# Loading `w_down` with one row in fourteen dealt apart: 13 rows per partition over all DMA engines, half of the last rows over four engines

## The chip, the core and the metric

The kernel runs on one core of a Trainium2 chip. The core has a matrix engine (PE), a vector engine (DVE), a scalar engine (ACT), GpSimd (POOL) and SyncE (SP), which here issues nearly all transfers; 16 DMA engines move the data from HBM to the on-chip memory of 128 partitions. The metric is device time in microseconds: the median of several executions.

## The reference

One decoding step for two rows `x` of 512 values: a layer norm, then attention over the last 4096 keys of a cache with 32 heads on 8 key heads, beside a gated feed-forward layer of width 1792; both are added to `x`. All is float32.

```python
x = A_x
xn = _layernorm(x, axis=-1)
return x + _A_ref(xn, A_k_cache, A_v_cache, A_wq, A_wo) + _B_ref(xn, B_W_gate, B_W_up, B_W_down)
...
def _A_ref(x, k_cache, v_cache, wq, wo):
    W = min(4096, max(256, Sk // 4))
    q = (x @ wq) ...                                # 32 heads of 128
    k, v = the last W keys and values, each for 4 heads
    p = _softmax(q k^T * (Dh ** -0.5), axis=-1)
    return (p v) @ wo
def _B_ref(x, W_gate, W_up, W_down):
    gate = jnp.einsum("bsd,df->bsf", x, W_gate)
    up = jnp.einsum("bsd,df->bsf", x, W_up)
    gate = gate * (gate > 0)
    h = gate * up
    return jnp.einsum("bsf,fd->bsd", h, W_down)
```

`W_down` has 1792 rows of 512 values, that is 2 KB each and 3.5 MB in all.

## The kernel before

Every weight and every piece of the caches is read once, 95 MB in all. SP issues the loads in the order of use: `wq` in two transfers of 4 MB, `W_gate` (`wg`) and `W_up` (`wu`) of 3.5 MB, sixteen transfers of 4 MB for keys (`k`) and values (`v`), then `W_down` (`wd`), and `wo` in a transfer of 4 MB and pieces of 2 MB, 1 MB, 512 KB and twice 256 KB. They go into a ring of four buffers (`RING`), so a load is issued when the load four places earlier has been used. Each transfer has 128 partitions as its outermost size. All these loads stand in one queue (q1 in the profile), one behind the other on each DMA engine.

SP, like every engine, runs its instructions in order; the kernel places them by hand (`manual_schedule`), and waits are put in where a tile's or a semaphore's earlier use asks for them. Transfers take eight semaphores in turn (DMAHW0 to DMAHW7 in the listings below), so the ninth takes the first one's again, once that transfer is known to be complete.

Early on, PE projects `x` to the queries and to gate and up; DVE multiplies those to `hh`, with four blocks of 448 of the 1792 columns one below the other, each on 32 partitions, and transposes it in blocks of 32 × 32 into `hT`, which has partition, row within the partition, and batch row. PE then works through scores (L259), softmax and values (L324) for eight key and value pieces, while DVE transposes the keys (L252, `kT`). At the end, after the last values, 14 matmuls `yw_ps<-wd,hT` (L422) take one row per partition of `wd` each, against the column of `hT` with the same index; eight small matmuls and a copy by ACT make `oT` from the last heads, and the matmuls on `wo` follow, the last ones (L426) piece by piece as the `wo` pieces land. DVE copies the sum to `yo` (L453), and SP and ACT write one row of the output each (L456).

In `load_down`, partition p holds rows 14p to 14p+13 of `W_down`, 28 KB in one stretch. So the `hT` column of partition p and index k belongs to feed-forward column 14p+k.

Of the kernel before, what the change touches and what calls it, by code (L numbers as in the profile page):

```python
# [9 lines left out]
F32 = mybir.dt.float32  # L10
# [10 lines left out]
def kernel(  # L21
# [12 lines left out]
    nc = tc.nc  # L34
    P = 128
    B, _, D = x.shape
# [18 lines left out]
    FB = F // P  # L55
# [4 lines left out]
    ring = ctx.enter_context(tc.tile_pool(name="ring", bufs=RING))  # L60
# [8 lines left out]
    def load(name, src, shape):  # L69
        t = ring.tile(shape, F32, name=name, tag="ring")  # L70
        nc.sync.dma_start(t, src)
        return t
# [6 lines left out]
    def load_ff(w, name):  # L79
        return load(name, w.rearrange("(p k) f -> p k f", p=P), [P, KC, F])  # L80

    def load_down():
        return load("wd", w_down.rearrange("(p k) e -> p k e", p=P), [P, FB, D])

    def load_kv(cache, name, g, a):
        r, b = divmod(g, B)
# [35 lines left out]
    hT = const.tile([P, FB, 32], F32, name="hT")  # L122
# [54 lines left out]
    for kc in range(KC):  # L177
        m, k = divmod(kc, 2)
# [12 lines left out]
    for kc in range(KC):  # L191
        for r in range(R):
            for c in range(C):
                n = r * C + c
# [6 lines left out]
    for r in range(R):  # L201
# [7 lines left out]
        for m in range(NB):  # L209
            src = qt[32 * m:32 * m + 32, :, :, 0].rearrange("p i (t h) b -> p b t h i", h=2)  # L210
            for x in range(Q):
                d = qz[32 * x:32 * x + 32, r * B:r * B + B, m]
                dst = bass.AP(
                    tensor=d.tensor, offset=d.offset + x * TK,
                    ap=[d.ap[0], d.ap[1], [64 + REP, NP], [32, 2], [1, REP]],
# [16 lines left out]
    nc.vector.scalar_tensor_tensor(gr, gs, 0.0, gs, op0=ALU.is_gt, op1=ALU.mult)  # L232
    hh = work.tile([P, FQ], F32, name="hh", tag="qs")
    nc.vector.tensor_tensor(hh, gr, u_ps, op=ALU.mult)
    nc.vector.transpose(hT, hh.rearrange("p (w k) -> p k w", k=FB))

# [161 lines left out]
    g = NG - 1  # L400
    vin = [load_kv(v_cache, "v", g, a) for a in range(NP)]
    dw = load_down()


# [80 lines left out]
```

## Time and profile before

| what | value |
|---|---|
| median of 3 runs | 230.34 us (230.26 to 230.57) |
| profiled execution: time, span | 230.8 us, 228.4 us |
| loads in queue q1 | 3896 packets, 94.90 MB, 97.0% of 16 DMA engines' span |
| mean DMA rate | 416 GB/s |
| PE, DVE, ACT busy | 63%, 49%, 12% of the span |
| granted PE clock, mean | 0.821 |
| chain that ended last: DMA, DVE, PE | 60%, 21%, 13% of the span |

The profiled execution is one of its own, 0.46 us above the median; its span runs from the first to the last instruction. In the rows below times stand in us from the start of the span. A row of the chain gives start, duration and the engine or transfer; a row of the DMA queues gives packets, MB and the time of the packets as a share of 16 engines over the span or window; the count "under 512 B" in the row on packets is, for queue q1, that of the completion packets of 4 B with which each DMA engine ends its part of a transfer. q8 and q14 are instruction fetches, q10 the queue of the transfers that ACT issues.

### The profile page before, as it was taken

What the parts mean: (1) busy time and instruction counts of PE and PEld (TensorE: products, weight loads), DVE (VectorE), ACT (ScalarE), POOL (GpSimd) and SP (SyncE); (2) the same over time, 40 slices, a digit from 0 to 9 for tenths busy, and PEclk for the clock granted to TensorE, in tenths of its full rate; (3) what the DMA queues carried; (4) which work ended last, traced back from release to release, by engine and by line L of the source; (5) the groups of instructions that cost most, each with busy time, mean ns of one, the idle gap of its engine ahead of it and who ended that gap; (6) DMA issues with size and microseconds to landing.
All of it is one profiled execution on the core that took longest, in us unless ns stands there. A gap on an engine that the chain in (4) does not pass through costs nothing.

```text
span 228.4 us, 2114 instructions
## 1 busy us (share of the span) xinstructions
PE 143.5 (63%) x864; PEld 40.1 (18%) x864; DVE 112.4 (49%) x176; ACT 27.0 (12%) x72; POOL 3.7 (2%) x11
## 2 busy tenths in 40 slices
PE   0582927806674038957499196859928757868393
PEld 0530211201111001402013011101401201214011
DVE  2300043049894499865992594797069272120000
ACT  2000123000000720003500000700000160000001
POOL 6000000000000000000000000000000000000000
PEclk9999767795999557997759859767995995999589
DMA  7999999999999999999999999999999999999991
GB/s 276 459 413 412 472 402 422 448 453 419 413 455 442 396 448 445 407 430 453 425 410 453 436 407 442 429 430 425 448 430 419 439 430 418 440 419 448 399 387 44
DMA packets 3917, 95.04 MB, mean 416 GB/s; under 512 B 442, under 2 KB 450, under 8 KB 836
## 3 DMA queue, kind: packets, MB, share of 16 engines
q1 hardware_dynamic: 3896, 94.90, 97.0%
q8 instruction: 7, 0.11, 0.2%
q14 instruction: 2, 0.02, 0.0%
q10 hardware_dynamic: 12, 0.01, 0.0%
HBM read 94.90 MB, written 0.00 MB: 416 GB/s over the span
## 4 chain that ended last, share of the span: by engine, by line
DMA 60%; DVE 21%; PE 13%; ACT 2%; issue 1%; SPq 1%; DVEq 0%; ACTq 0%
DMA k<-in_A_k_cache_dram 39%; DVE kT L252 16%; DMA wo<-in_A_wo_dram 11%; DMA wq<-in_A_wq_dram 9%; PE s L259 5%; PE o L324 4%; PE q_ps L195 2%; DVE pt L304 2%; ACT pz L291 1%; DVE pT L297 1%; DVE on L333 1%; PE oa L344 1%; SPq L441 1%; DVE m L271 1%; ACT L291 1%
## 5 line engine op out<-in xcount | busy, mean ns | idle before, releaser
L259 PE MATMUL s<-kT,qz 128*32 128x512 f32 x256 | 61.5, 780 | 43.7 <-DVE kT L252 43.7
L252 DVE STREAM_TRANSPOSE kT<-k 128x1024 f32<-128x1024 f32 x64 | 73.5, 1210 | 19.9 <-DMA k<-in_A_k_cache_dram 19.8
L324 PE MATMUL o<-v,pt 128*32 128x512 f32 x256 | 36.6, 677 | 0.0
L259 PEld LDWEIGHTS s<-kT,qz 128*32 128x32 f32 x256 | 10.7, 127 | 88.3 <-DVE kT L252 47.5
L344 PE MATMUL oa<-on,pick 128*16 128x512 f32 x16 | 12.5, 876 | 4.5 <-DVE on L333 4.5
L291 ACT ACTIVATE pz<-s,nm 64x512 f32<-64x512 f32 x8 | 5.8, 726 | 74.6 <-DVE nm L285 74.5
L195 PE MATMUL q_ps<-wq,xnT 128*32 128x512 f32 x64 | 10.9, 846 | 4.9 <-DMA wq<-in_A_wq_dram 4.9
L324 PEld LDWEIGHTS o<-v,pt 128*32 128x32 f32 x256 | 10.5, 122 | 19.9 <-issue 19.7
L304 ACT COPY pt<-pT 32x256 f32<-32x256 f32 x32 | 12.8, 401 | 5.6 <-DVE pT L297 5.2
L217 DVE COPY qz<-qt 32x32 f32<-32x32 f32 x16 | 3.0, 188 | 21.1 <-ACT qz L217 21.1
L422 PE MATMUL yw_ps<-wo,oT 128*2 128x512 f32 x56 | 8.1, 730 | 4.4 <-DMA wo<-in_A_wo_dram 4.4
L333 DVE TENSOR_TENSOR on<-o,own_u 128x512 f32<-128x512 f32 x8 | 5.4, 673 | 10.8 <-PE o L324 10.8
L453 DVE COPY yo<-y_ps 128x128 f32<-128x128 f32 x1 | 0.3, 292 | 20.2 <-PE y_ps L426 20.2
L304 DVE COPY pt<-pT 32x256 f32<-32x256 f32 x32 | 9.1, 285 | 0.5
L297 DVE STREAM_TRANSPOSE pT<-pz 128x1024 f32<-128x1024 f32 x4 | 5.0, 1246 | 8.3 <-ACT pz L291 8.3
L183 PE MATMUL xt_ps<-rep,xc 2*128 2x32 f32 x16 | 3.7, 402 | 8.4 <-DVE rep L176 8.4
L271 DVE TENSOR_REDUCE m<-s 128x1 f32<-128x512 f32 x4 | 2.8, 692 | 8.5 <-PE s L259 8.5
L225 PE MATMUL u_ps<-wu,xnT 128*32 128x448 f32 x32 | 4.8, 764 | 2.2 <-DMA wu<-in_B_W_up_dram 2.2
L291 ACT ACT_TABLE_LOAD x1 | 1.3, 1283 | 34.6 <-DVE nm L285 34.6
L183 PEld LDWEIGHTS xt_ps<-rep,xc 2*128 2x128 f32 x16 | 3.6, 319 | 8.4 <-DVE rep L176 8.4
L225 PE MATMUL g_ps<-wg,xnT 128*32 128x448 f32 x32 | 5.0, 783 | 0.0
L195 PEld LDWEIGHTS q_ps<-wq,xnT 128*32 128x32 f32 x64 | 2.7, 147 | 12.1 <-issue 6.2
(69 smaller groups left out, 56.5 us busy)
## 6 DMA issues: line engine op xcount, KB each, us to landing
k<-in_A_k_cache_dram SPq DMA_DIRECT2D x8, 4096.0 KB, 29.5
v<-in_A_v_cache_dram SPq DMA_DIRECT2D x8, 4096.0 KB, 29.2
wq<-in_A_wq_dram SPq DMA_DIRECT2D x2, 4096.0 KB, 16.7
wo<-in_A_wo_dram SPq DMA_DIRECT2D x1, 4096.0 KB, 29.7
wg<-in_B_W_gate_dram SPq DMA_DIRECT2D x1, 3584.0 KB, 29.4
wu<-in_B_W_up_dram SPq DMA_DIRECT2D x1, 3584.0 KB
wd<-in_B_W_down_dram SPq DMA_DIRECT2D x1, 3584.0 KB
wo<-in_A_wo_dram SPq DMA_DIRECT2D x1, 2048.0 KB, 22.9
```

Source lines behind the costliest of these rows:

```text
L183: nc.tensor.matmul(xt_ps[:, v, kc, :], lhsT, rep16.rearrange("r s b -> r (s b)"), start=True, stop=True)
L195: nc.tensor.matmul(q_ps[r][32 * c:32 * c + 32, :], xnT[:, 0, kc, :], wqt[kc // 2][:, kc % 2, n * 512:(n + 1) * 512], start=(kc == 0), stop ...
L225: nc.tensor.matmul(dst[32 * c:32 * c + 32, :], xnT[:, 1, kc, :], wt[:, kc, c * FQ:(c + 1) * FQ], start=(kc == 0), stop=(kc == KC - 1),)
L252: nc.vector.transpose(kt[:, c * n:(c + 1) * n].rearrange("p j m i -> p j (m i)"), src[:, c * n:(c + 1) * n])
L259: nc.tensor.matmul(ss[g][32 * q:32 * q + 32, :], qz[:, g, 2 * mh + m, a, h], kt[:, JS * s1:JS * s1 + JS, m, h::2], start=(a == 0 and mh == ...
L291: nc.scalar.activation(pv[o, :, :, h], ss[g][o].rearrange("p (j i) -> p j i", j=JS), AF.Exp, bias=nm[o], scale=SCALE, accum_out=l[o],)
L297: nc.vector.transpose(pT.rearrange("p j x t k -> p (j x t k)"), pz.rearrange("p j s -> p (j s)"))
L304: (nc.vector.tensor_copy if n % 2 else nc.scalar.copy)(pts[g][32 * x:32 * x + 32, :, s1, :, h], pT[q:q + 32, :, x].rearrange("p j t k -> p ...
L324: nc.tensor.matmul(o[32 * q:32 * q + 32, :], pts[g][:, a, s1, j:j + 4].rearrange("p u h k -> p (u h k)"), v[:, lo:lo + 512], start=(s1 == ...
L333: nc.vector.tensor_tensor(ons[a], o.rearrange("p (u d) -> p u d", u=4), own_u[:, :, None].to_broadcast([P, 4, P]), op=ALU.mult)
L344: nc.tensor.matmul(oa[g].rearrange("h u d -> h (u d)"), pick[:, 8 - 8 * a:24 - 8 * a], ons[a].rearrange("p u d -> p (u d)"), start=(a == 0 ...
L422: nc.tensor.matmul(yw_ps[32 * c:32 * c + B, :], lhsT, w, start=(n < Q), stop=(n >= wide - Q))
```

## The change

`W_down` is seen as 32 runs of 56 rows; four partitions share one run. Each partition gets 13 rows in one stretch (26 KB) from the first 52 rows of its run, by a transfer over 128 partitions. The last four rows of a run go to its four partitions, one each. These last rows come by five more transfers: four of 4 runs (16 rows, 32 KB in all, each with outermost size 4), and one of 16 runs (64 rows, 128 KB, outermost size 16). The bytes stay the same. The transpose of `hh` becomes two, one for the 13 rows and one for the last, to match.

```diff
+    FM = FB - 1
+    PR = 4
+    RUN = PR * FB
+
     def load_down():
-        return load("wd", w_down.rearrange("(p k) e -> p k e", p=P), [P, FB, D])
+        t = ring.tile([P, FB, D], F32, name="wd", tag="ring")
+        nc.sync.dma_start(
+            t[:, 0:FM], bass.AP(tensor=w_down.tensor, offset=w_down.offset, ap=[[RUN * D, P // PR], [FM * D, PR], [1, FM * D]])
+        )
+        n = 0
+        for m in [4] * 4 + [16]:
+            src = bass.AP(
+                tensor=w_down.tensor, offset=w_down.offset + (n * RUN + PR * FM) * D, ap=[[RUN * D, m], [D, PR], [1, D]]
+            )
+            nc.sync.dma_start(t[n * PR:(n + m) * PR, FM], src)
+            n += m
+        return t
...
-    nc.vector.transpose(hT, hh.rearrange("p (w k) -> p k w", k=FB))
+    hr = hh.rearrange("p (i n) -> p i n", n=RUN)
+    nc.vector.transpose(
+        hT[:, 0:FM].rearrange("p k (i j) -> p k i j", j=PR), hr[:, :, 0:PR * FM].rearrange("p i (j k) -> p k i j", k=FM)
+    )
+    nc.vector.transpose(hT[:, FM].rearrange("p (i j) -> p i j", j=PR), hr[:, :, PR * FM:RUN])
```

On SP, from the last two `v` loads to the output's write, this stood before (line, operation, tile and source, shape, and in brackets the semaphores waited for: DMAHW0 to DMAHW7 of earlier transfers, PE and DVE of those engines' work):

```order
L71 DMA v_0_798<-in_A_v_cache_dram 128x1x8192 [waits DMAHW7_49,DVE_49]
L71 DMA v_1_800<-in_A_v_cache_dram 128x1x8192 [waits DMAHW0_49,PE_49]
L71 DMA wd<-in_B_W_down_dram 128x7168 [waits DMAHW1_49,DVE_49]
L441 DMA wo_884<-in_A_wo_dram 128x8192 [waits DMAHW2_49,PE_49]
L441 DMA wo_886<-in_A_wo_dram 128x4096 [waits DMAHW3_49,PE_49]
L441 DMA wo_886<-in_A_wo_dram 128x2048
L441 DMA wo_886<-in_A_wo_dram 128x1024
L441 DMA wo_886<-in_A_wo_dram 128x512 x2
L456 DMA out_dram<-yo 4x128 [waits DMAHW5_49,DVE_49]
```

On SP in the same place, after the change:

```order
L71 DMA v_0_799<-in_A_v_cache_dram 128x1x8192 [waits DMAHW7_49,DVE_49]
L71 DMA v_1_801<-in_A_v_cache_dram 128x1x8192 [waits DMAHW0_49,PE_49]
L88 DMA wd<-in_B_W_down_dram 128x1x6656 [waits DMAHW1_49,DVE_49]
L96 DMA wd<-in_B_W_down_dram 16x1x512 x4
L96 DMA wd<-in_B_W_down_dram 64x1x512 [waits DMAHW2_49]
L460 DMA wo_890<-in_A_wo_dram 128x8192 [waits DMAHW3_49,PE_49]
L460 DMA wo_892<-in_A_wo_dram 128x4096 [waits DMAHW4_49,PE_49]
L460 DMA wo_892<-in_A_wo_dram 128x2048 [waits DMAHW5_49]
L460 DMA wo_892<-in_A_wo_dram 128x1024 [waits DMAHW6_49]
L460 DMA wo_892<-in_A_wo_dram 128x512 [waits DMAHW7_49]
L460 DMA wo_892<-in_A_wo_dram 128x512 [waits DMAHW0_49]
```

Five transfers have come in behind the first one of `wd`, and with five more semaphores taken the `wo` transfers now wait for the completion of the last two `v` loads (DMAHW3, DMAHW4), and the last four pieces for that of the large `wd` transfer (DMAHW5) and of its first three small ones (DMAHW6, DMAHW7, DMAHW0).

On PE, at the end, from the last softmax sum to the first matmuls on `wo`, after the change:

```order
L332 MATMUL lp_859<-l_749,by_h 16x1
L441 MATMUL yw_ps<-wd,hT 2x512 [waits DMAHW5_49]
L441 MATMUL yw_ps<-wd,hT 2x512 x12
L441 MATMUL yw_ps<-wd,hT 2x512 [waits DMAHW6_49,DMAHW2_49,DMAHW7_49,DMAHW1_49,DMAHW0_49]
L381 MATMUL op_880<-osb_793,spread 128x32 [waits DVE_49]
L381 MATMUL op_880<-osb_793,spread 128x32 x7
L441 MATMUL yw_ps<-wo_890,oT 2x512 [waits DMAHW3_49]
```

Before, the first of the 14 matmuls on `wd` waited for the one transfer and the other 13 for none; now the last of them waits for the five small transfers. On DVE the one transpose into `hT` is two, in the same place.

## The prediction

> **What bounds the kernel now.** I read the page's queues and chain first, then the chain in order of time at its end, then the DMA share in narrow windows.
>
> ```profile
> q1 hardware_dynamic: 3896, 94.90, 97.0%
> DMA 60%; DVE 21%; PE 13%; ACT 2%; issue 1%; SPq 1%; DVEq 0%; ACTq 0%
> 198.46 26.13 DMA wo<-in_A_wo_dram
> 224.59 0.04 issue
> 224.64 0.45 PE y_ps L426 x8
> 225.11 0.29 DVE yo L453
> ```
>
> Queue q1 (all loads) keeps the 16 DMA engines busy for 97.0% of the span, and the chain ends in the landing of the last piece of `wo`, with only 0.45 us of PE and 0.29 us of DVE before the output's write. So the end is set by the DMA engine that finishes its share last. The chain's DVE and PE shares lie earlier, where queued loads keep the engines fed. The windows at the end say how uneven the engines are (columns: window, its length, busy us of PE, PEld, DVE, ACT, POOL, clock, DMA share, GB/s).
>
> ```profile
> 222.10:222.60 0.50, 0.50 (x8) 0.11 (x8) 0.00 (x0) 0.00 (x0) 0.00 (x0) 1.00 0.78 303
> 222.60:223.10 0.50, 0.50 (x8) 0.00 (x0) 0.00 (x0) 0.00 (x0) 0.00 (x0) 1.00 0.48 184
> 223.50:224.00 0.50, 0.50 (x24) 0.29 (x16) 0.00 (x0) 0.30 (x1) 0.00 (x0) 1.00 0.38 147
> 224.20:224.70 0.50, 0.33 (x16) 0.06 (x8) 0.00 (x0) 0.00 (x0) 0.00 (x0) 1.00 0.00 0
> ```
>
> Share times 16 is engines at work: 0.48 is eight, 0.38 is six, and after 224.2 none. Six engines finish some 1.8 us after the first eight. Every load through q1 is cut evenly over 16 engines, so something else made six late. Next, the DMA view in narrow windows: each engine ends its part of a transfer with one tiny completion packet (the column "under 512 B"), so counting these tells when engines finish. Windows 36.8 to 37.9, 38.5 to 39.2 and 40.3 to 40.6 (the end of `wu`), then 202.3 to 203, 203.3 to 203.8 and 203.8 to 204.7 (the end of `wd`), then the page's rows of other queues:
>
> ```profile
> q8 instruction: 1, 0.02, 5.9%
> DMA packets 30, 0.49 MB, mean 702 GB/s; under 512 B 15, under 2 KB 15, under 8 KB 15
> DMA packets 3, 0.07 MB, mean 218 GB/s; under 512 B 1, under 2 KB 1, under 8 KB 1
> ...
> DMA packets 22, 0.42 MB, mean 603 GB/s; under 512 B 8, under 2 KB 8, under 8 KB 8
> DMA packets 11, 0.27 MB, mean 549 GB/s; under 512 B 2, under 2 KB 2, under 8 KB 2
> DMA packets 18, 0.39 MB, mean 437 GB/s; under 512 B 6, under 2 KB 6, under 8 KB 6
> ...
> q8 instruction: 7, 0.11, 0.2%
> q14 instruction: 2, 0.02, 0.0%
> ```
>
> The instruction fetch takes 5.9% of 16 engines for 1.1 us, that is 1.04 us of one engine, and behind it fifteen engines end `wu` in time and one over a microsecond late. A late engine never catches up, since all carry equal bytes. By the end of `wd`: eight in time, two from 203.3 on, six from 203.8 on. Of the seven q8 fetches one comes after 224.2 (window 224.2 to 226.6, row below); six before it and six late engines, two q14 fetches and two middling ones: every fetch met another engine.
>
> ```profile
> q8 instruction: 1, 0.02, 2.6%
> ```
>
> [...]
>
> **The change, part by part.** The price of bytes comes from the steady stretch 27.9 to 60.4, that of a 2 KB packet from 223.5 to 224.0, whether a small transfer uses few engines from the page's q10.
>
> ```profile
> q1 hardware_dynamic: 511, 13.99, 100.0%
> DMA packets 38, 0.07 MB, mean 147 GB/s; under 512 B 2, under 2 KB 2, under 8 KB 38
> q1 hardware_dynamic: 38, 0.07, 38.0%
> q10 hardware_dynamic: 12, 0.01, 0.0%
> ```
>
> *Removed on every engine.* The large transfer carries 13 rows per partition instead of 14: 2 KB less on each of the eight partitions of an engine, 16,384 B. 13.99 MB in 32.5 us over 16 engines is 26.9 GB/s each, so 0.61 us less.
>
> *Added on every engine.* The transfer of 16 runs brings 64 rows, four per engine. 38.0% of 16 engines for 0.5 us is 3.04 us, for 36 data packets and two completions: at most 84 ns per 2 KB. Four: 0.34 us. Net 0.27 us less on twelve engines.
>
> *Added on four engines.* Four transfers of 16 rows, if each runs on four engines, bring 16 rows to each: 16 × 84 ns = 1.34 us. Net of the first two terms, 1.1 us more. No row shows a load of outer size 4, but q10 comes near: its 12 packets are ACT's load of `x` (2 rows) and its store of 4 rows, each row with one completion, so outer size 2 used two engines and 4 used four. The bounds of a row are 76 ns (2,048 B at 26.9 GB/s) and 84 ns; I take 84, of the same size. If an engine stopped between pieces, it would be dearer (third rival).
>
> *Which four.* No view numbers the engines. I take it that a transfer starts them in the order of their numbers, so the lowest are those that start and finish first. In windows 11.97 to 12.19 (end of the first load), 202.43 to 202.67 (end of `wd`) and 222.12 to 222.34 (last piece) the first four completions stand:
>
> ```profile
> DMA packets 8, 0.13 MB, mean 596 GB/s; under 512 B 4, under 2 KB 4, under 8 KB 4
> DMA packets 10, 0.19 MB, mean 785 GB/s; under 512 B 4, under 2 KB 4, under 8 KB 4
> DMA packets 32, 0.07 MB, mean 326 GB/s; under 512 B 4, under 2 KB 4, under 8 KB 32
> ```
>
> Four in the first 0.22 us at the start, four in the first 0.24 us after all fetches: the leaders kept their lead, so none of the four first starters was met. [...]
>
> *Sum.* Twelve engines: 224.2 − 0.27 = 223.93 for the six late ones. The four: the latest of them completes before 222.34, plus 1.1 = 223.45. The late ones still end last, 0.48 us behind the four, and the chain behind the landing is unchanged: the profiled 230.8 (span 228.4 and 2.4 around it) becomes 230.53. It lies 0.46 above the median, so the median 230.34 becomes 230.07; I say 230.1. Even with ideal balance only 0.27 us can come, since the late engines lose no more.
>
> *SP's queue.* Five more issues, and waits for older transfers whose semaphores are taken again.
>
> ```profile
> 177.09 0.34 SPq L71 DMA_DIRECT2D wd<-in_B_W_down_dram  x1
> 185.00 0.33 SPq L441 DMA_DIRECT2D wo<-in_A_wo_dram  x1
> 196.67 2.23 SPq L441 DMA_DIRECT2D wo<-in_A_wo_dram  x5
> SPq L441 <- PE o L324: 17.4, 2, 9.9
> DVE kT L252 <- DMA k<-in_A_k_cache_dram: 19.8, 4, 8.7
> ```
>
> Five issues of 0.43 us (2.23 / 5 is 0.45 with gaps) are 2.2 us, inside the 7.6 us in which SP waits before 185.0. Then the first `wo` transfer waits for the second-last load of `v` as well, whose stragglers complete by about 186.4 (their `wd` end, 204.7 at most, less one 4 MB load of 9.75 us and one `wd` of 8.53 us, both from bytes at 26.9 GB/s): 1.4 us later, with `v` and `wd` still queued, so free. The four last `wo` pieces are now held until the parts of `wd` landed, about 204.6 instead of 197 to 199. At that moment each engine holds most of the 32 KB packets of the first `wo` transfer (9.7 us) and the 2 MB piece (4.9 us), issued before: the next piece is needed after 217. Cover about 12 us; without it every microsecond of wait would be one of idle engines.
>
> *PE and DVE.* The last matmul on `wd` waits for five transfers more. Queued behind it are the eight `op` matmuls and ACT's copy, which have room before the `wo` wait, and the transpose to `hT` becomes two in front of the first `kT`:
>
> ```profile
> PE yw_ps L422 <- DMA wo<-in_A_wo_dram: 4.4, 2, 4.1
> 46.51 0.94 DVE L235 STREAM_TRANSPOSE hT<-hh 128x448 f32<-128x448 f32 x1
> 50.66 1.25 DVE L252 STREAM_TRANSPOSE kT<-k 128x1024 f32<-128x1024 f32 x1 [3.21 <-DMA k<-in_A_k_cache_dram]
> ```
>
> The four engines end `wd` at 202.67 + 1.1 = 203.8, ahead of the late ones, so PE starts no later; and 4.1 us lie free before `wo`. The transposes may take from 0.9 to four times as long before the 3.21 us of idle DVE is used up. Both cost nothing.
>
> **Rivals.** *First, one of the four lowest engines is a late one* (engines start in another order, or the fetches meet other engines in each execution). Then 224.2 + 1.1 = 225.3 sets the end, 1.1 us later: 231.4. An early engine may end as late as 223.1 now before 1.1 us more costs time; past that it decides. Against it: the leaders' windows; for it, that start order is all I have for numbers, and one execution. With a middling engine, which ends by 223.5, 224.6 at most: 230.4 to 230.7.
>
> [...]
>
> *Third, small pieces do not stream.* If the four engines stop after each for as long as from the last packet to PE's release (224.2 to 224.6, 0.4 us), five stops add 2.0 to 223.45: 225.45, hence 231.6. Against it stands window 221.4 to 222.2, in which 2 KB pieces and 17 completions passed and the engines stayed full:
>
> ```profile
> q1 hardware_dynamic: 134, 0.31, 100.6%
> ```
>
> [...]
>
> *Fourth, the four-run transfers go over all engines*, one row each: −0.61 + 8 × 0.084 = 0.06 more everywhere, with completions 0.1: 230.4. Against it: q10.
>
> **How the numbers follow.** Forecast 0.64, own range 229.8 to 230.5 (the 0.27 and the ±0.2 of the shown runs). Late engine among the four, or level engines, 0.23; a middling one 0.05; pieces that stop 0.02; all engines 0.03; something else that is faster 0.03. A measurement here tells 0.2%, 0.46 us, from no change, and the forecast's 0.27 is less. Faster: 0.03 and the forecast's edge 0.06. Slower: 0.25. The rest is same. Leaving out the first rival would leave out more than 2 in 10, so the range reaches to 231.5.
>
> **What would show it.** In the trace after: the last engines done at 223.9 instead of 224.2; about twelve of 16 at work from 222.6 to 223.1 (eight before); the last completions of `wd`'s small pieces near 203.8; SP's last four `wo` issues after 204, with a DMA share of 1.0 up to 222. Wrong would be: a last landing near 225.3 with four engines or fewer at work ahead of it, a dip in the share near 217, or a seventh instruction fetch that moves before 223.5 and meets an engine still loading.

## The result, and the profile after

The changed kernel takes 232.05 us (median of 6, 231.88 to 232.58) against 230.44 us (median of 6) before: a ratio of 1.0072, interval 1.0059 to 1.0085, that is 1.6 us slower. The prediction had 230.1 and a range up to 231.5. The profiled execution took 232.21 us, with a span of 230.1.

The chain in order of time still ends in the landing of the last `wo` piece, now at 226.25 instead of 224.59; what follows it is as long as before:

```profile
206.82 19.43 DMA wo<-in_A_wo_dram
226.29 0.45 PE y_ps L445 x8
226.76 0.29 DVE yo L472
```

The windows of the end (DMA share in the column before the last):

```profile
222.60:223.10 0.50, 0.50 (x12) 0.10 (x4) 0.00 (x0) 0.00 (x0) 0.00 (x0) 1.00 1.01 397
223.50:224.00 0.50, 0.50 (x8) 0.11 (x8) 0.00 (x0) 0.00 (x0) 0.00 (x0) 1.00 0.63 246
225.00:225.50 0.50, 0.48 (x16) 0.32 (x16) 0.00 (x0) 0.49 (x1) 0.00 (x0) 1.00 0.20 78
225.50:226.00 0.50, 0.50 (x24) 0.31 (x16) 0.00 (x0) 0.00 (x0) 0.00 (x0) 1.00 0.04 16
```

Before, eight engines were at work from 222.6 to 223.1 (share 0.48); now all sixteen are (1.01). Everything is late, the early engines too. Where that happened is seen in one window, 202.5 to 206.0, in which the end of `wd` passes. First before, then after:

```profile
202.50:206.00 3.50, 1.95 (x16) 0.55 (x20) 1.18 (x4) 0.00 (x0) 0.00 (x0) 1.00 1.01 428
...
202.50:206.00 3.50, 1.00 (x12) 0.25 (x13) 1.02 (x3) 0.00 (x0) 0.00 (x0) 1.00 1.02 310
```

The DMA share is full in both (1.01 and 1.02), and the rate has fallen from 428 to 310 GB/s. The engines are as busy as ever, and each byte takes longer. (428 − 310) GB/s × 3.5 us is 0.41 MB not moved, or 0.96 us of the whole stream in this window alone. From 207 on the rate is normal again (418 GB/s in 207 to 222, 410 before in 207 to 221).

Durations of single packets, read from the trace's records (all pieces of 2 KB between 200 and 210; packets of 32 KB that started between 203 and 205):

```
kernel                                     2 KB: count, mean, longest ns    32 KB: count, mean, longest ns
before                                       -                              19, 1239, 1687 (one beside a fetch)
after                                      128, 114, 169                    12, 1773, 1844
one transfer of 128 partitions             128,  84,  95                    20, 1226, 1247
two transfers of 64 partitions             128, 110, 232                    16, 1506, 1742
four pieces to partitions 0-15, 32-47       64,  85,  93                    22, 1219, 1246
two pieces to partitions 0-31, 32-63        64,  84,  86                    23, 1223, 1241
four pieces to partitions 64-79, 96-111     64, 148, 194                    12, 2178, 2339
four pieces to partitions 16-31, 48-63      64, 148, 187                    12, 2003, 2216
```

The pieces cost 114 ns on average after the change, not 84, and the 32 KB packets of the first `wo` transfer, which the change does not touch, took 1.77 us on average while the pieces passed; before, those that started in the same two microseconds took 1.24 (1.21 without the one beside a fetch).

### The profile page after: what moved, and what is told of

It is laid out like the page before. It is cut to its first block, busy times and chain, and to the rows that moved or that the text cites. A ratio compares the mean times of both kernels' runs of the same rounds, so it can differ in the third digit from the quotient of the medians.

```text
span 230.1 us, 2122 instructions
## 1 busy us (share of the span) xinstructions
PE 136.0 (59%) x864; PEld 39.2 (17%) x864; DVE 112.3 (49%) x177; ACT 27.1 (12%) x72; POOL 3.7 (2%) x11
## 4 chain that ended last, share of the span: by engine, by line
DMA 69%; DVE 21%; PE 6%; ACT 1%; issue 1%; SPq 1%; DVEq 0%; ACTq 0%
DMA k<-in_A_k_cache_dram 39%; DVE kT L271 17%; DMA wd<-in_B_W_down_dram 12%; DMA wq<-in_A_wq_dram 9%; DMA wo<-in_A_wo_dram 8%; PE q_ps L210 2%; PE s L278 2%; PE o L343 2%; DVE pt L323 1%; DVE on L352 1%; ACT pz L310 1%; ACT L310 1%; DVE pT L316 1%; SPq L460 1%; DVE m L290 0%
## 5 line engine op out<-in xcount | busy, mean ns | idle before, releaser
L278 PE MATMUL s<-kT,qz 128*32 128x512 f32 x256 | 60.8, 765 | 49.2 <-DVE kT L271 49.2
L343 PE MATMUL o<-v,pt 128*32 128x512 f32 x256 | 33.0, 616 | 0.0
L210 PE MATMUL q_ps<-wq,xnT 128*32 128x512 f32 x64 | 10.4, 808 | 5.7 <-DMA wq<-in_A_wq_dram 5.7
L363 PE MATMUL oa<-on,pick 128*16 128x512 f32 x16 | 10.6, 750 | 4.5 <-DVE on L352 4.5
L441 PE MATMUL yw_ps<-wd,hT 128*2 128x512 f32 x28 | 3.6, 592 | 2.5 <-DMA wd<-in_B_W_down_dram 2.5
L240 PE MATMUL u_ps<-wu,xnT 128*32 128x448 f32 x32 | 3.2, 542 | 2.9 <-DMA wu<-in_B_W_up_dram 2.9
```

What stands on the lines that cost most here:

```text
L210: nc.tensor.matmul(q_ps[r][32 * c:32 * c + 32, :], xnT[:, 0, kc, :], wqt[kc // 2][:, kc % 2, n * 512:(n + 1) * 512], start=(kc == 0), stop ...
L240: nc.tensor.matmul(dst[32 * c:32 * c + 32, :], xnT[:, 1, kc, :], wt[:, kc, c * FQ:(c + 1) * FQ], start=(kc == 0), stop=(kc == KC - 1),)
L278: nc.tensor.matmul(ss[g][32 * q:32 * q + 32, :], qz[:, g, 2 * mh + m, a, h], kt[:, JS * s1:JS * s1 + JS, m, h::2], start=(a == 0 and mh == ...
L343: nc.tensor.matmul(o[32 * q:32 * q + 32, :], pts[g][:, a, s1, j:j + 4].rearrange("p u h k -> p (u h k)"), v[:, lo:lo + 512], start=(s1 == ...
L363: nc.tensor.matmul(oa[g].rearrange("h u d -> h (u d)"), pick[:, 8 - 8 * a:24 - 8 * a], ons[a].rearrange("p u d -> p (u d)"), start=(a == 0 ...
L441: nc.tensor.matmul(yw_ps[32 * c:32 * c + B, :], lhsT, w, start=(n < Q), stop=(n >= wide - Q))
```

## Experiments

Two theories stood after this. *Crossing*: a transfer over 128 partitions would give each DMA engine certain partitions, a smaller transfer would give an engine other ones, and two engines would write the same part of the on-chip memory at once. *Rows*: 2 KB rows at a distance of 114,688 B, or the 26 KB stretches, are slow to read. A third, *four*: nothing but four engines with more to carry. Six kernels with times tell them apart; four runs of three more kernels, with marks, tell which engines are early. No run shows which engine writes which partition, nor an engine's number: which partitions belong to which engine, and what crosses, is the theory's, in the expectations as below, and the "lowest" engines are those that a small transfer uses. The four kernels with two or four pieces compute other sums over `wd`, as their expectations say; the loads are what counts.

**One transfer of 128 partitions for the last rows**

```diff
-        for m in [4] * 4 + [16]:
+        for m in [32]:
```

> The last rows come by one transfer over all 128 partitions instead of five small ones; everything else as after the change. Theory 'crossing' (the small transfers write partitions that in a 128-partition load belong to another DMA engine, and two engines on one place slow each other and their neighbours): nothing crosses here, so before's time plus about 0.1 us, 230.5, and no dip of the rate near 203 to 206. Theory 'rows' (2 KB rows out of a stretch of 114,688 B, or the 26 KB stretches, read slowly wherever they go): the dip stays, 231.5 to 232. Theory 'four' (the four engines are simply late, nothing else): 230.5.

230.45 us against 230.37, ratio 1.000 (0.9991 to 1.001). The 128 rows are the same 2 KB rows from the same places, the 13-row stretches and the two transposes too, and nothing is lost. In the window 202.5 to 206.0:

```profile
202.50:206.00 3.50, 1.48 (x16) 0.42 (x20) 0.66 (x2) 0.00 (x0) 0.00 (x0) 1.00 1.10 463
```

*Rows* falls.

**Two transfers of 64 partitions, each over all engines**

```diff
-        for m in [4] * 4 + [16]:
+        for m in [16, 16]:
```

> The last rows come by two transfers of 64 partitions, each over all 16 engines, four rows per engine each; no transfer over four engines. [...] 'Rows': 231.5 to 232. 'Four': no engine has more than another, 230.5.

231.28 us against 230.37, ratio 1.0033 (1.002 to 1.0047). No engine carries more than another: in the changed kernel the packets under 512 B are 32 more than before, 474 against 442, as four completions for each transfer of 16 rows and 16 for the one of 64 make it. Still it is slower, with a dip:

```profile
202.50:206.00 3.50, 1.96 (x16) 0.55 (x20) 1.63 (x4) 0.00 (x0) 0.00 (x0) 1.00 1.07 355
```

*Four* alone cannot explain this.

**Four pieces over four engines, written to partitions 0 to 15 and 32 to 47**

```diff
+    PIECES = ((0, 14), (32, 14), (0, 15), (32, 15))     # first partition, column of the tile
+    MAIN = FB * D - D // 2                              # 13.5 rows
...
+        for n, (p0, col) in enumerate(PIECES):
+            src = bass.AP(
+                tensor=w_down.tensor, offset=w_down.offset + (n * 4 * 56 + 52) * D, ap=[[56 * D, 4], [D, 4], [1, D]]
+            )
+            nc.sync.dma_start(t[p0:p0 + 16, col], src)
```

> The kernel before with its w_down transfer cut to 13.5 rows per partition, and four pieces of 16 rows over the four lowest engines behind it, written to partitions 0 to 15 and 32 to 47 (its sums over w_down are not the reference's; the bytes and the order of the loads are those of the changed kernel). 'Crossing': these partitions are the four engines' own, no dip; twelve engines carry 0.30 us less and four 1.04 us more: 230.1 if the four are early ones, 231.4 if one of them had an instruction fetch. 'Rows': a dip as after the change, over 231.5. 'Four': 231.4 to 232.

230.53 us against 230.37, ratio 1.0006 (0.9997 to 1.0015): between the two values that were expected, and the packets keep their durations, 85 ns and 1.22 us. The rate in the window is 400 GB/s, at a share of 0.94. Followed record by record (each packet starts on its engine 4 to some 15 ns before the recorded end of the one ahead of it), five of the six late engines end at 223.62 to 223.99, earlier than the 224.04 to 224.18 of before, but the sixth at 224.20 and the last engine with pieces at 224.42.

**The same, written to partitions 64 to 79 and 96 to 111**

```diff
-    PIECES = ((0, 14), (32, 14), (0, 15), (32, 15))
+    PIECES = ((64, 14), (96, 14), (64, 15), (96, 15))
```

> As the run with partitions 0 to 15 and 32 to 47, with the four pieces written to partitions 64 to 79 and 96 to 111 (sums over w_down not the reference's). 'Crossing': these belong to other engines, so the rate dips while the pieces pass, and it is slower than the run before it by 0.5 to 1.5 us. 'Rows' and 'four': the same time as that run, within 0.2 us.

232.70 us against 230.37, ratio 1.0094 (1.0075 to 1.0114), 2.2 us slower than its twin. Its row and the twin's, the twin first:

```profile
202.50:206.00 3.50, 0.98 (x12) 0.32 (x16) 0.88 (x3) 0.00 (x0) 0.00 (x0) 1.00 0.94 400
...
202.50:206.00 3.50, 1.06 (x4) 0.30 (x4) 1.43 (x4) 0.00 (x0) 0.00 (x0) 0.88 1.11 274
```

Same bytes from the same addresses, same sizes, same number of engines and order; only the partitions written differ, and with them those that PE reads. That PE isn't the cause is seen in the chains. In both, the chain's end runs over PE, not over the last piece of `wo`: the 4 MB `wo` transfer lands, 56 matmuls on it follow, then ACT's copy and the last matmuls. The twin first again:

```profile
186.84 28.11 DMA wo<-in_A_wo_dram
215.00 8.80 PE yw_ps L434 x56
...
185.12 32.08 DMA wo<-in_A_wo_dram
217.24 8.70 PE yw_ps L434 x56
```

The transfer lands at 217.20 instead of 214.95, 2.2 us later, and the matmuls behind it take no longer. 128 KB in such pieces cost 2.2 us. The cost was larger than the 0.5 to 1.5 us expected, because it isn't confined to a few engines: all twelve 32 KB packets that started between 203 and 205 took 2.01 to 2.34 us. Followed record by record, ten of them are of ten engines that carry no piece; two are of engines that were done with their pieces. Nor is a piece slow merely because of the partitions that it is written to: the first ten took 84 or 85 ns, as the twin's do, and those from the eleventh on 94 to 194.

**The same, written to partitions 16 to 31 and 48 to 63**

```diff
-    PIECES = ((0, 14), (32, 14), (0, 15), (32, 15))
+    PIECES = ((16, 14), (48, 14), (16, 15), (48, 15))
...
+        nc.gpsimd.memset(t[0:64, FB:FB + 2], 0.0)
```

> As the run with four pieces to partitions 0 to 15 and 32 to 47, with the pieces written to partitions 16 to 31 and 48 to 63 (sums over w_down not the reference's; GpSimd clears the two spare columns first). [...] 'Crossing': slow like the pieces to partitions 64 to 111, 232 to 233, with a dip of the rate near 203 to 206. If only the upper and lower half of the partitions matter: as the pieces to 0 to 15 and 32 to 47, 230.5.

232.81 us against 230.51, ratio 1.0101 (1.0085 to 1.0116):

```profile
202.50:206.00 3.50, 0.00 (x0) 0.00 (x0) 0.78 (x2) 0.00 (x0) 0.00 (x0) 0.95 0.98 253
```

So it isn't a matter of the two halves of the partitions. (GpSimd's clearing was over by 178.3, long before the pieces moved.) Over four engines, pieces to partitions 0 to 15 and 32 to 47 took 85 ns, and those to 16 to 31 and 48 to 63, like those to 64 to 79 and 96 to 111, 148 ns: the three kernels agree with *crossing* if in the loads around them these four engines write partitions 0 to 15 and 32 to 47 and none of the others. No run shows that, and none shows two engines at one place. Nor does a run show why engines without a piece slow down.

**Two pieces over eight engines, to partitions 0 to 31 and 32 to 63**

```diff
-    PIECES = ((0, 14), (32, 14), (0, 15), (32, 15))
+    PIECES = ((0, 14), (32, 14))
...
-                tensor=w_down.tensor, offset=w_down.offset + (n * 4 * 56 + 52) * D, ap=[[56 * D, 4], [D, 4], [1, D]]
+                tensor=w_down.tensor, offset=w_down.offset + (n * 8 * 56 + 52) * D, ap=[[56 * D, 8], [D, 4], [1, D]]
...
-            nc.sync.dma_start(t[p0:p0 + 16, col], src)
+            nc.sync.dma_start(t[p0:p0 + 32, col], src)
```

> w_down with 13.5 rows per partition over all engines and two pieces of 32 rows, each over the eight lowest engines, to partitions 0 to 31 and 32 to 63 (sums over w_down not the reference's). Nothing crosses: engines 0 to 7 carry 0.37 us more, the others 0.30 less. If all six late engines are among 8 to 15: 230.1; if one is among 0 to 7: 230.8. A dip or 231 and more would speak against 'crossing'.

230.44 us against 230.51, ratio 0.9995 (0.9986 to 1.0005). No dip (451 GB/s in the window), hence the eight engines were loaded apart without harm, and without a gain that can be measured. The pieces to partitions 16 to 31 and 48 to 63 took 84 ns here and 148 ns over four engines, so these partitions are not slow to write; it is argued from this that it matters which engine writes them. Neither 230.1 nor 230.8 came: followed record by record, the six late engines were all among those without pieces, and five of them ended earlier than before or level with it, but the last at 224.22, no sooner than the 224.18 of before.

**Marks: which engines are early.** Five tiny transfers behind `wd`, of k rows each (544 to 800 B a row), run on k engines. Engines are numbered by these marks alone: 0 and 1 have the mark of two rows, 2 is the one that the mark of three adds, and so on; that a mark takes the same engines in each kernel and execution is assumed.

```diff
+        for k in counts:
+            nc.sync.dma_start(
+                t[0:k, at:at + n], bass.AP(tensor=w_down.tensor, offset=w_down.offset, ap=[[D, k], [1, n]])
+            )
```

> The kernel before with ten tiny transfers as marks: five at the start and five behind the w_down transfer, of 2, 3, 4, 8 and 12 rows, each of a size of its own (240 to 784 B a row). [...] My reading of the prediction (the lowest four start first and meet no fetch): engines 0 to 3 pass within 0.35 us of the first. The reading of the runs after the change ('two early, two a little late'): two of engines 0 to 3 pass about 1 us after the first two. If fetches meet other engines in each execution, the places differ from the run beside it. The time: 230.5 to 232, not of use here.

> As the run beside it, with marks behind w_down alone, of 5, 6, 7, 10 and 14 rows: they part engines 0 to 4, 5, 6, 7 to 9, 10 to 13 and 14 to 15. If the instruction fetches meet the same engines in every execution, the six late and the two middling engines have the places that the other run gives them; if not, not. The time: 230.4 to 231.

> The run with marks of 5, 6, 7, 10 and 14 rows once more, unchanged. If the fetches meet the same engines in every execution of a kernel, the same places come late again: one early-numbered pair of 0 to 4, engine 5, engines 10 to 13, with 14 and 15 early. If the place moves from execution to execution, other engines are late.

> Marks of 2, 3, 4, 8 and 12 rows behind w_down alone, without the five at the start. If the places are fixed by the kernel's code they are those of the run with 5, 6, 7, 10 and 14 rows, whose code differs only in the marks' shapes: engines 4, 6, 7, 8 and 9 early, 14 and 15 early. If not, another set of six.

Each k gave k packets and k completions (in the second execution with 5, 6, 7, 10 and 14 rows, 42 packets of 512 B to 2 KB between 202.4 and 205, and 58 smaller ones: 42, and 16 of `wd`), and the engines of a smaller mark are among those of the next larger one. So the packets can be followed from mark to mark, and engines told apart by the marks that they lack. Their first marks (us, from the records; those in one group are not told apart):

```
marks of 2, 3, 4, 8, 12 (also at the start): 0-1: 204.04 204.69 | 2: 203.82 | 3: 204.76 | 4-7: 203.76 203.91 203.92 203.98 | 8-11: 203.89 204.02 205.32 205.54
marks of 2, 3, 4, 8, 12:                     0-1: 202.63 203.53 | 2: 202.75 | 3: 203.66 | 4-7: 202.54 202.73 202.77 204.36 | 8-11: 202.87 203.01 204.49 204.50
marks of 5, 6, 7, 10, 14:  0-4: 202.58 202.65 202.72 203.49 204.05 | 5: 204.36 | 6: 202.98 | 7-9: 202.87 203.02 203.18 | 10-13: 204.35 204.38 204.54 204.57
the same kernel again:     0-4: 202.53 202.60 202.67 203.53 204.16 | 5: 204.25 | 6: 202.65 | 7-9: 202.68 203.18 203.29 | 10-13: 204.34 204.44 204.49 204.80
```

In both kernels that part 0 and 1, 2, and 3, two of the four engines with the mark of four are 0.7 to 1.0 us behind the other two, as the second reading in the expectation had it. The kernel that ran twice, the second time on another chip, had the same engines late both times, in the groups that its marks part, and the one with marks of 2, 3, 4, 8 and 12 behind `wd` alone agrees with it (one late among 4 to 7, two among 8 to 11); the kernel with marks at the start, whose code differs most, had none of 4 to 7 late. What sets the places was not tried. The times, of one execution each in the order of the rows, are 231.24, 230.45, 230.51 and 230.67 us.

## Why the prediction was wrong, step by step

**The price of a small piece: the step that failed first.** The prediction took 84 ns for 2 KB from the last `wo` pieces, which are parts of transfers over 128 partitions, "of the same size", never asked where a piece is written, and took it that the other engines go on as before. Two of the changed kernel's five small transfers write to partitions 16 to 31 and 48 to 63, where pieces over four engines took 148 ns in the experiment, and the largest takes 64 partitions over sixteen engines, as the pieces of 110 ns do. A piece took 114 ns on average, and the 32 KB packets beside the pieces 1.77 us instead of 1.24. The kernels with pieces to partitions 64 to 79 and 96 to 111 and to 0 to 15 and 32 to 47, 232.70 against 230.53, price the crossing at 2.2 us for 64 rows over four engines; the kernel at 232.81 belongs to another series and is 2.3 us above the before of that. For the transfers of 64 partitions over sixteen engines it is 0.9 us (231.28 against 230.37). In the changed kernel the difference to the uncrossed pieces is 232.05 − 230.53 = 1.5 us; that this is the crossing is argued, since the two also differ in how many rows come in small transfers. To the kernel with the same rows in one transfer it is 232.05 − 230.45 = 1.6 us, for the crossing and the load of the four engines together. No rival had it: the third one, pieces that stop, had a dearer engine but not a slower neighbour, and its 0.4 us per piece is not what happened, since the engines stayed full (share 1.02).

**Which four: wrong as well.** Start order was taken for engine order, and the four engines of a small transfer for the lowest; no run shows an engine's number, or which numbers a small transfer takes. Whether the same four lead in all three windows, counts of completions can't tell; the four engines that carry the pieces are not four early ones. In the uncrossed twin, two of them end the large `wd` transfer at 202.25 and 202.47 and two at 203.15 and 203.42. In the changed kernel it is 202.10 and 202.33, 203.38 and 203.62, and their pieces end at 204.31, 204.57, 205.68 and 205.97, where 203.8 was forecast. That two had met a fetch is inferred from this lateness and from the marks. It is the middling engine of the first rival, priced at 230.4 to 230.7, and the uncrossed twin came out there: 230.53, its last 2 KB packet ending at 224.42 where before the last ended at 224.18. In the changed kernel the last two engines to finish (225.6 and 225.8) are two of the four; the other two of them end at 224.7 and 224.8, six engines without pieces from 224.8 to 225.3, the remaining six from 223.2 to 223.6. Without crossing the twin was about 0.2 us slower than before; by that, some 1.4 us of the 1.6 are left for the crossing, an estimate from two kernels and not a measured split.

**The gain on the late engines: not seen.** Five of the six late engines of the twin ended earlier than before, by 0.2 to 0.4 us in order of their ends, as the 0.27 us less on twelve engines would have it; but the last engine without pieces ended at 224.20 there and at 224.22 in the kernel with eight engines, against 224.18 before. The end hangs on the latest of six, which is not the same amount late in each execution. PE left little room as well. Before, its last matmuls waited for the last piece until 224.64; started right behind ACT's copy at 223.85 and taking 0.90 us as in the kernel with one transfer of 128 partitions, they would have ended 0.3 us earlier at most (an estimate). In the twin, and in that kernel, PE ended the chain. (In the sum, 222.34 + 1.1 is 223.44, not 223.45, which changes nothing.)

**What the late engines come from: right.** One fetch, one engine, 1.04 us (between 36.8 and 37.9 before), never regained: the rate and the shares of the windows stand, and the marks show six late engines in the same places twice. Level engines were not seen in any trace; of executions without the profiler there is none.

**The bytes: right.** With pieces that don't cross, the shares and times came as summed: one transfer of 128 partitions 230.45, where 0.06 us more was expected of its bytes.

**SP, PE and DVE: right for the changed kernel.** SP issued the first `wo` transfer at 187.09 and the last four pieces after the parts of `wd`, its last at 207.2, and the engines stayed full until then and after (share 1.02 in 202.5 to 206, 0.98 in 207 to 222).

```profile
187.09 0.35 SPq L460 DMA_DIRECT2D wo<-in_A_wo_dram  x1
196.79 10.45 SPq L460 DMA_DIRECT2D wo<-in_A_wo_dram  x5
PE yw_ps L441 <- DMA wo<-in_A_wo_dram: 5.4, 1, 5.4
45.30 0.89 DVE L251 STREAM_TRANSPOSE hT<-hh 128x416 f32<-128x416 f32 x1
46.12 0.17 DVE L254 STREAM_TRANSPOSE hT<-hh 128x32 f32<-128x32 f32 x1
```

The matmuls on `wd` began 0.4 us later than before, at 205.52, and PE then had 5.4 us to wait for `wo`; the two transposes take 0.04 us longer from the end of `hh` than the one did before.

**The range** reached to 231.5 for a late engine among the four. What came was that in a mild form and the crossing on top, so the likeliest number and the sign were off, and the range too short by 0.6 us.

**Open:** why engines without a piece slow down too (32 KB packets of 2.18 us on average beside the pieces, 1.22 in the twin), and whether two engines meet on one place at all; and whether a division of bytes that follows the late engines would gain. The version over eight engines was the one tried, and was the same as before (ratio 0.9995).

## What to carry to other kernels

Before cutting a large load into smaller transfers, time the pieces at several groups of partitions, and read the durations of the packets beside them as well: 128 KB in pieces over four engines cost 2.2 us more at one group than at another here (232.70 against 230.53), although the engines look fully busy, and the 128 last rows in one transfer of 128 partitions nothing that can be measured (ratio 1.000). Look at what the chain does behind the transfer, too: where PE is nearly as late as the last landing, a better balance of the load engines has little to give (0.3 us at most here, the estimate above). When a DMA-bound stretch grows, compare the rate at equal share: here a full share with a lower rate (1.02 and 310 GB/s, after 1.01 and 428) meant packets that became slower (1.77 us for 32 KB instead of 1.24), not engines that wait. And which engines a small transfer will use is not to be read off the order in which packets start; marks of a few rows tell more.

## What the runs showed of the hardware that was not expected

- Four pieces of 32 KB over four engines, written to partitions 64 to 79 and 96 to 111 instead of 0 to 15 and 32 to 47, raised the 32 KB packets that started in two microseconds beside them, ten of the twelve on engines without a piece, from 1.22 us to 2.18 us on average, and cut the core's rate from 400 to 274 GB/s in a window of 3.5 us. The first ten pieces themselves still took 84 or 85 ns.
- A transfer of 64 partitions over 16 engines beside 128-partition loads cost time as well: 355 GB/s in the window and 0.9 us for two of 128 KB.
- In two executions of one kernel, on two chips, the same load engines were late (10 to 13, 5 and two of 0 to 4, numbered by the marks), and partly others in another kernel; one instruction fetch held one engine for 1.04 us.
